# A third buffer for 64-bit weight rows, another place for the second quad, and new numbers for the transfer planner

## The chip, the cores and the metric

One core of a Trainium2 chip runs the whole program in one launch. The metric is device time in microseconds (us); shorter is better. Engines are named as in the profile: PE is TensorE, DVE VectorE, ACT ScalarE, POOL GpSimd, SP SyncE. SP issues all the transfers of this kernel.

## The reference

Attention with a sigmoid in place of the softmax, then two feed-forward layers, over 4 × 448 = 1792 tokens:

```python
scores = scale * np.matmul(q, k.transpose(0, 1, 3, 2)) - np.log(S)   # 4 x 12 heads, S = 448, dim 64
attn = 1.0 / (1.0 + np.exp(-scores))
x = (attn @ v) with the heads side by side                            # 1792 x 768
h = x @ w_in;  x = (s * np.maximum(h, 0.0) ** 2 + b) @ w_out          # layer 1, d_ff 2048
h = x @ w_in2
out = (np.maximum(h, 0.0) + alpha * np.minimum(h, 0.0)) @ w_out2      # layer 2
```

The tokens are float32. The four weight matrices come as float64; they are turned into float32 on the chip, and this conversion is a good part of what the other engines and the transfers do.

## The kernel before, in words

**Phases.** Attention runs until about 136 us, on tiles of 64 × 64, with TensorE multiplying (L857, L895) and ScalarE computing a sigmoid (L873) for each. Then come layer 1 and layer 2, each for two groups of tokens: in, out, in, out, about 103 us each. The first of these, in of layer 1 for the first group, is `first_phase` (about 136 to 245 us): eight blocks `mp` of 7 × 9 = 63 matmuls. The later ones are `in_phase` and `out_phase`.

**Strassen.** Each layer multiplies by Strassen and Winograd's scheme of seven products (M1 to M7) on 2 × 2 blocks. The left operand of a product is one of seven combinations of weight blocks, A11, A12, A22 and S1 to S4. Each float32 operand is split into a high part (ACT, L450, a CAST) and a low part (DVE, L453, a difference), and three matmuls (L547 to L549) stand for one.

**From float64 to a quad.** `quad()` makes the seven combinations for one block. Two loads (L328) bring two rows of 64-bit weights, 768 KB each (512 KB for some), into the two buffers of R64, `r640` and `r641`. For each row ACT runs a Prelu on the high words (L362), DVE joins high and low words into float32 (L365 TENSOR_SCALAR, L370 SCALAR_TENSOR_TENSOR), and DVE forms four sums (L383). The seven results lie side by side in a quad buffer, `quada`, `quadb` or `quadc`, and are stored to DRAM (L402 for in-blocks, L411 for out-blocks: `w0out<-quada`). Later phases load them back as raw units of 512 KB (`raw0`, `raw1`, L328) and split them into `ring`. The first phase doesn't wait for that way round: `direct()` splits straight out of a quad into four buffers `rinq`. Its even blocks stand in quadb, its odd ones in quada. Out-quads of layer 1 that are made early (seven in attention, two inside the first phase) all go through quada.

**Memory.** `quadb` lies over raw0, raw1 and the first part of `neg` (a scratch tensor of layer 2); `quadc` lies at the start of neg.

**The order of the work.** The program first records all operations in `Plan.add`, each with its engine, an estimated duration, a latency, and what it reads and writes. `Plan.order` computes for each the latest start that lets TensorE keep its own order without waiting (`late`), and `Plan.place` then lays the operations down one by one: of what is ready, on the engine that is free first, the one that can start first, and among equals the one due first. It repeats this three times (`ROUNDS`), with TensorE's starts of one pass as the goals of the next. A transfer is reckoned at 345 GB/s (`dma_t`, L314) and a latency of 2.2 us. Loads and stores share one pipe and SP's order. TensorE's own order is fixed as the program records it.

Two kinds of dependence count. Cells of 64 floats give the true ones. Beside them, buffers whose memory overlaps are treated as one by the framework that emits the waits: who comes later in the laid order waits for the last one before it that wrote an overlapping buffer, also where the cells differ. `behind()` (L118) lets the planner reckon with that for an operation which it is about to place, not for those that come after it.

**Buffers of the trace.** `g` holds a layer's result between products, with `L558` (ACT copies out of PSUM), `L568` and `L576` (DVE adds PSUM to g), `L594` (relu), `L629` and `L632` (square, then scale and bias) working on it. `sg` is a sigmoid's result, `x` and `xo` the tokens, `gb` the split g.

Of the kernel before, what the change touches and what calls it, by code (L numbers as in the profile page):

```python
# [16 lines left out]
P = 128  # L17
NWARM = 6
CELL = 64
QUEUES = {"SP": 0.07, "POOL": 1.0}  # L20
AHEAD = 1.0
ROUNDS = 3
SAFE = 0.0
PIPE = {"DVE": 0.08, "ACT": 0.09}
EARLY = 7
# [29 lines left out]
class Plan:  # L55
# [57 lines left out]
    def place(self, succ, late, pe):  # L113
        n = len(self.ops)
        share = self.shared()
        wrote, used = ([{} for _ in share] for _ in range(2))

        def behind(i, eng):  # L118

            x = 0.0  # L120
            for mine, of in zip(self.uses[i], (wrote, used)):
                for t in mine:
                    for o in share[t]:
                        for e, at in of[o].items():
                            if at > x and e != eng:
                                x = at
            return x
        left = [len(op[3]) for op in self.ops]
        est = [0.0] * n
        pe_at = 0  # L130
        open_ = {}
        for i in range(n):
            if left[i] == 0:
                open_.setdefault(self.ops[i][0], set()).add(i)
        free, done, at = {}, [], {}
        pipe = 0.0
        while len(done) < n:
            best = None
            for eng, cand in open_.items():
                if not cand:  # L140
                    continue
                f = free.get(eng, 0.0)
                if eng in QUEUES:
                    f = max(f, pipe - AHEAD)
                if eng == "PE":
                    i = pe[pe_at]
                    if i not in cand:
                        continue
                    est[i] = max(est[i], behind(i, eng))
                    pick = (max(f, est[i]), late[i], i)  # L150
                else:
                    while True:
                        pick = min((max(f, est[i]), late[i], i) for i in cand)
                        i = pick[2]
                        x = behind(i, eng)
                        if x <= pick[0]:
                            break
                        est[i] = x
                if best is None or pick < best[0]:
                    best = (pick, eng)  # L160
            (start, _, i), eng = best
            open_[eng].discard(i)
            if eng == "PE":
                pe_at += 1
            dur, lat = self.ops[i][1:3]
            if eng in QUEUES:
                free[eng] = start + QUEUES[eng]
                pipe = max(pipe, start) + dur
                end = pipe
            else:  # L170
                end = free[eng] = start + dur
            at[i] = start
            done.append(i)
            for k, mine in enumerate(self.uses[i]):
                for t in mine:
                    for of in (used, wrote)[: k + 1]:
                        of[t][eng] = max(of[t].get(eng, 0.0), end + lat)
            for s in succ[i]:
                est[s] = max(est[s], end + (lat if self.ops[s][0] != eng else 0.0) + PIPE.get(eng, 0.0))
                left[s] -= 1  # L180
                if left[s] == 0:
                    open_.setdefault(self.ops[s][0], set()).add(s)
        return done, at
# [26 lines left out]
def tile_kernel(  # L210
# [13 lines left out]
    nc = tc.nc  # L224
    B, NPR, _, SKQ = kq.shape
# [15 lines left out]

    NSLOT = 37
    NRING, NRAW, NTMP = 3, 2, 7
    UNIT = 8 * P
    WQ = KH * P
    base0 = -(-nc.sbuf_base // (4 * CELL)) * CELL
# [5 lines left out]
    def take(n):  # L252
        nonlocal at
        a = at
        at += -(-n // CELL) * CELL
        return a

    def tensor(name, base, n, dtype=F32):
        t = nc.alloc_sbuf_tensor_at(name, [P, n], dtype, offset=4 * base)
        plan.tensors.append((base, base + n))  # L260
        return Ref(t.ap(), base, len(plan.tensors) - 1)

    def own(name, n):
# [1 line left out]

    SLOTS = take(NSLOT * SLOT)
    RING0 = take(NRING * 2 * UNIT)
    PROD = take(8 * WQ + 7 * WQ)
    SPARE = take(NRAW * UNIT + 7 * WQ)
    RING = [tensor(f"ring{i}", RING0 + i * 2 * UNIT, 2 * UNIT, F32R) for i in range(NRING)]  # L270
    RING4 = [tensor(f"rinq{i}", RING0 + i * 4 * WQ, 4 * WQ, F32R) for i in range(4)]
# [1 line left out]
    NEG = tensor("neg", SPARE + NRAW * UNIT, 2 * S)  # L273
# [6 lines left out]
        [(tensor("xraw12", MID + 2 * SLOT + XB, XB), 0, XB)],  # L280
        [(tensor("xraw13", MID + XB, S), 0, S), (tensor("xraw14", NEG.base, 2 * S), S, XB)],
    ]
    R64 = [tensor(f"r64{i}", PROD + 4 * WQ * i, 4 * WQ) for i in range(2)]
    QUADS = [
        tensor("quada", PROD + 8 * WQ, 7 * WQ),
        tensor("quadb", SPARE, 7 * WQ),
        tensor("quadc", NEG.base, 7 * WQ),
    ]
    TMP = [own(f"tmp{i}", S) for i in range(NTMP)]
    SMALL = take(CELL)  # L290
# [21 lines left out]
        return 0.08 + 0.53e-3 * n  # L312

    def dma_t(n):  # L314
        return n * 4 * P / 345e3

    DMA_LAT = 2.2
    PE_LAT = 0.25
# [16 lines left out]
    def quad(m, kind, k, c, place=0):  # L335
# [11 lines left out]
        for row in range(2):  # L347
            src = w64[m, kind][2 * k + row]
            if kind == "out":
                src = src[:, 2 * c0 * P : 2 * c1 * P]  # L350
            r64 = R64[row]
            raw = sb(r64, 4 * n).bitcast(U32)
            load(raw, src.bitcast(U32), 4 * n, (), cells(r64, 4 * n), DMA_LAT + SAFE)
            v = raw.rearrange("p (b n t) -> p b n t", b=2, t=2)
# [57 lines left out]
            cells(QUAD, 7 * n), wrote, DMA_LAT,  # L412
        )

    n_unit = [0, 0]
    ring = {}

    def entry(chunks, ring_=RING):
# [535 lines left out]
    def produce(n, both=False):  # L954
        for i in range(min(n, len(quads))):
            m, kind, k, c, *place = quads.pop(0)
            quad(m, kind, k, c, *(place or [2 * (i % 2) if both else 0]))

    for u in range(NU + 2):
        if u < NU:  # L960
# [89 lines left out]
```

## Time and profile before

| what | us |
|---|---|
| runs | 966.35, 966.47, 974.77 |
| median of the runs | 966.47 |
| the profiled execution | 970.06 |
| its span in the trace | 968.3 |

The span goes from the first to the last instruction in the trace; the execution's own time is 1.76 us longer. The profile has one line per instruction or group, with its start, its duration and, in square brackets, how long the engine had been idle before it and what ended that idle time. `x8` means eight alike in one line. Matmuls overlap in the pipe, so the distance of their starts says more than their durations.

### The profile page before, as it was taken

The page shows a single profiled execution, that of the slowest core. Times are in us where ns is not written, and L with a number is a line of the kernel's source. Part 1 is how long each engine was busy: PE and PEld are TensorE (multiplying, and loading weights), DVE is VectorE, ACT ScalarE, POOL GpSimd, SP SyncE. Part 2 cuts the span into 40 slices and gives each one's busy share as a digit, 9 for nine tenths or more (in the row PEclk, how much of TensorE's full clock was granted, in tenths as well). Part 3 has the DMA queues.
Part 4 walks back from the last instruction along what each step waited for, and adds up shares of the span by engine and source line. Part 5 has one row for each costly group of instructions (what it writes and reads, how often), then busy time and mean ns, then how long its engine had stood idle before and what let it go on. Part 6 is the DMA issues. An engine that isn't in the chain of part 4 may idle for free.

```text
span 968.3 us, 13904 instructions
## 1 busy us (share of the span) xinstructions
PE 954.7 (99%) x5424; PEld 810.4 (84%) x5424; DVE 729.6 (75%) x862; ACT 653.1 (67%) x793; POOL 0.2 (0%) x4
## 2 busy tenths in 40 slices
PE   9999999999999999999999999999999999999998
PEld 4343458988899999998999999999999999999997
DVE  2567648997995877788898969789968556699661
ACT  6989967788945546889946547677555466676451
POOL 0000000000000000000000000000000000000000
PEclk9999999999999999999999999999999999999999
DMA  8999978886663479997567787766444443333441
GB/s 277 343 329 330 348 253 283 291 279 251 213 207 109 145 237 333 311 334 264 190 185 225 252 333 274 247 215 217 148 134 150 138 117 107 103 109 119 133 146 66
DMA packets 81106, 211.68 MB, mean 219 GB/s; under 512 B 7184, under 2 KB 45840, under 8 KB 81040
## 3 DMA queue, kind: packets, MB, share of 16 engines
q1 hardware_dynamic: 81040, 210.80, 65.6%
q8 instruction: 42, 0.69, 0.3%
q14 instruction: 24, 0.20, 0.1%
HBM read 152.97 MB, written 57.80 MB: 218 GB/s over the span
## 4 chain that ended last, share of the span: by engine, by line
PE 67%; DVE 11%; DMA 10%; ACT 8%; issue 3%; SPq 0%; DVEq 0%; ACTq 0%
PE ps L547 20%; PE ps L548 20%; PE ps L549 20%; PE ps L857 4%; DMA w0out<-quada 4%; PE ps L895 3%; DMA r<-in_w_in 3%; DMA r<-in_w_out 3%; DVE ring L453 2%; DVE quada L383 1%; ACT g L629 1%; ACT g L632 1%; DVE quada L370 1%; DVE gb L453 1%; ACT ring L450 1%
## 5 line engine op out<-in xcount | busy, mean ns | idle before, releaser
L547 PE MATMUL ps<-gb,ring 128*128 128x448 f32 x672 | 245.8, 366 | 1.3 <-DVE gb L453 1.3
L549 PE MATMUL ps<-gb,ring 128*128 128x448 f32 x672 | 245.5, 365 | 0.6 <-DVE ring L453 0.6
L548 PE MATMUL ps<-gb,ring 128*128 128x448 f32 x672 | 245.4, 365 | 0.0
L453 DVE TENSOR_TENSOR ring<-raw,ring 128x1024 fp32r<-128x1024 f32 x147 | 179.5, 1221 | 76.5 <-ACT ring L450 76.5
L450 ACT CAST ring<-raw 128x1024 fp32r<-128x1024 f32 x147 | 154.1, 1048 | 100.3 <-PE ps L548 77.5
L547 PE MATMUL ps<-xo,ring 128*128 128x448 f32 x504 | 184.5, 366 | 0.4 <-DVE tmp L568 0.3
L549 PE MATMUL ps<-xo,ring 128*128 128x448 f32 x504 | 184.3, 366 | 0.0
L548 PE MATMUL ps<-xo,ring 128*128 128x448 f32 x504 | 184.3, 366 | 0.0
L547 PEld LDWEIGHTS ps<-gb,ring 128*128 128x128 f32 x672 | 126.2, 188 | 12.5 <-DVE gb L453 2.4
L549 PEld LDWEIGHTS ps<-gb,ring 128*128 128x128 f32 x672 | 126.2, 188 | 11.0 <-DVE ring L453 1.0
L548 PEld LDWEIGHTS ps<-gb,ring 128*128 128x128 f32 x672 | 126.2, 188 | 9.9
L453 DVE TENSOR_TENSOR gb<-g,gb 128x1344 fp32r<-128x1344 f32 (+1 forms) x84 | 116.7, 1399 | 15.2 <-ACT gb L450 13.6
L450 ACT CAST gb<-g 128x1344 fp32r<-128x1344 f32 (+1 forms) x84 | 99.5, 1193 | 25.2 <-PE ps L549 14.6
L547 PEld LDWEIGHTS ps<-xo,ring 128*128 128x128 f32 x504 | 94.6, 188 | 9.0 <-DVE tmp L568 0.6
L549 PEld LDWEIGHTS ps<-xo,ring 128*128 128x128 f32 x504 | 94.7, 188 | 7.8
L548 PEld LDWEIGHTS ps<-xo,ring 128*128 128x128 f32 x504 | 94.7, 188 | 7.8
L873 ACT ACTIVATE sg<-ps,bias 128x896 f32<-128x896 f32 x84 | 83.2, 1010 | 14.7 <-PE ps L857 14.1
L362 ACT ACTIVATE r<-r 128x768 f32<-128x768 f32 (+1 forms) x68 | 59.3, 873 | 42.1 <-DMA r<-in_w_out 23.0
L857 PE MATMUL ps<-kq 64*64 64x448 f32 x672 | 79.6, 548 | 2.8 <-ACT sg L873 2.7
L895 PE MATMUL ps<-sg,v 64*64 64x448 f32 x672 | 77.9, 536 | 0.0
L568 DVE TENSOR_TENSOR g<-ps,g 128x448 f32<-128x448 f32 x104 | 63.5, 620 | 17.3 <-ACT g L558 10.5
L547 PE MATMUL ps<-xo,rinq 128*128 128x448 f32 x168 | 62.5, 372 | 3.8 <-DVE g L568 2.2
(51 smaller groups left out, 994.5 us busy)
## 6 DMA issues: line engine op xcount, KB each, us to landing
r<-in_w_in SPq DMA_DIRECT2D x32, 768.0 KB, 5.9
raw<-w0out SPq DMA_DIRECT2D x42, 512.0 KB, 3.7
raw<-w1in SPq DMA_DIRECT2D x42, 512.0 KB, 3.6
raw<-w1out SPq DMA_DIRECT2D x42, 512.0 KB, 3.6
r<-in_w_out SPq DMA_DIRECT2D x24, 768.0 KB, 5.7
raw<-w0in SPq DMA_DIRECT2D x21, 512.0 KB, 5.7
kq<-in_qk SPq DMA_DIRECT2D x23, 448.0 KB, 5.4
w0out<-quada SPq DMA_DIRECT2D x6, 1344.0 KB, 7.9
```

The costliest lines, as they stand in the source:

```text
L362: nc.scalar.activation(hi, hi, AF.Prelu, scale=2.0**-112, alpha=-(2.0**32))
L370: nc.vector.scalar_tensor_tensor(out=u, in0=hi.bitcast(U32), scalar=3, in1=u, op0=ALU.logical_shift_left, op1=ALU.bitwise_or,)
L383: lambda: nc.vector.tensor_tensor(out=o_, in0=x_, in1=y_, op=op),
L450: add("ACT", act_t(n), lambda: nc.scalar.copy(h, x), cells(src, n), cells(hi, n))
L453: lambda: nc.vector.tensor_tensor(out=l, in0=x, in1=h.bitcast(F32), op=ALU.subtract),
L547: nc.tensor.matmul(d, wh_, ml_, start=first and k == 0, stop=False, **opt)
L548: nc.tensor.matmul(d, wh_, mh_, start=False, stop=False, **opt)
L549: nc.tensor.matmul(d, wl_, mh_, start=False, stop=last and k == n, **opt)
L568: lambda: nc.vector.tensor_tensor(out=d, in0=bank(k), in1=o, op=ALU.add),
L857: nc.tensor.matmul(ps[h * D : (h + 1) * D, k + j, :S], a.ap[rows, S + k0 : S + k0 + D], a.ap[rows, :S], start=True, stop=True,)
L873: lambda: nc.scalar.activation(o, i, AF.Sigmoid, bias=sb(BIAS, 1), scale=QKSCALE),
L895: nc.tensor.matmul(ps[j * D : (j + 1) * D, k + h, :S], va[keys, v : v + D], a.ap[keys, j * S : (j + 1) * S], start=first, stop=last,)
```

## The change

1. R64 gets a third buffer (`NR64 = 3`), and rows take the three in turn instead of one buffer for each of the two rows. The 6 KB of each partition come out of the scratch space for dynamic transfers, which is cut to 1024.
2. `quadb` moves to the start of neg, off the raw units' memory, and `quadc` is gone. Where quads alternate, they alternate between quada and quadb.
3. The planner reckons with 319.4 GB/s instead of 345 and makes one pass instead of three.
4. On SP, an operation that would be picked is set aside when another operation, recorded earlier and not yet placed, uses an overlapping buffer and is due before the transfer would have ended and 4 us more have passed (`POLITE`, `SLACK`, `ahead`).

```diff
+POLITE = ("SP",)
+SLACK = 4.0
-ROUNDS = 3
+ROUNDS = 1
+DMA_RATE = 319.4e3
...
+        def ahead(i, end):
+
+            for mine, of in zip(self.uses[i], open_uses[::-1]):
+                for t in mine:
+                    for o in share[t]:
+                        if any(j < i and late[j] < end for j in of[o]):
+                            return True
+            return False
...
-                        if x <= pick[0]:
-                            break
-                        est[i] = x
+                        if x > pick[0]:
+                            est[i] = x
+                            continue
+                        if eng in POLITE:
+                            dur, lat = self.ops[i][1:3]
+                            x = max(pick[0], pipe) if eng in QUEUES else pick[0]
+                            if ahead(i, x + dur + lat + SLACK):
+                                cand = cand - {i}
+                                if not cand:
+                                    pick = None
+                                    break
+                                continue
+                        break
...
+    NR64 = 3
...
-    PROD = take(8 * WQ + 7 * WQ)
+    PROD = take((4 * NR64 + 7) * WQ)
...
-        tensor("quada", PROD + 8 * WQ, 7 * WQ),
-        tensor("quadb", SPARE, 7 * WQ),
-        tensor("quadc", NEG.base, 7 * WQ),
+        tensor("quada", PROD + 4 * NR64 * WQ, 7 * WQ),
+        tensor("quadb", NEG.base, 7 * WQ),
...
-        return n * 4 * P / 345e3
+        return n * 4 * P / DMA_RATE
...
-            r64 = R64[row]
+            r64 = R64[n_unit[2] % NR64]
+            n_unit[2] += 1
...
-            quad(m, kind, k, c, *(place or [2 * (i % 2) if both else 0]))
+            quad(m, kind, k, c, *(place or [i % 2 if both else 0]))
...
-    nc = bacc.Bacc("TRN2", target_bir_lowering=False, num_devices=1)
+    nc = bacc.Bacc("TRN2", target_bir_lowering=False, num_devices=1, dynamic_dma_scratch_size=1024)
```

The lines of the changed file are 34 or 35 higher than those of the file before (L328 becomes L362, L365 L400, L370 L405, L383 L418, L453 L488, L568 L603). The number of instructions and TensorE's order stay as they are. Three places show what moves.

**SP at the start of attention.** Before, rows 14 to 22 of SP. `r640` and `r641` are the row buffers, `in_w_in1` and `in_w_out1` the weights of layer 1; kq and v are attention's inputs, sc, bc and al small constants:

```order
L328 DMA r641_77<-in_w_in1 128x1536
L328 DMA sc_89<-in_s 128x1
L328 DMA v2_142<-in_vt 128x512
L328 DMA bc_90<-in_b 128x1
L328 DMA al_92<-in_alpha 128x16
L328 DMA r640_76<-in_w_out1 128x1536
L328 DMA kq3_134<-in_qk 128x896
L328 DMA r641_77<-in_w_out1 128x1536
L328 DMA v3_143<-in_vt 128x512
```

and now the same rows:

```order
L362 DMA r642_78<-in_w_out1 128x1536
L362 DMA v2_142<-in_vt 128x512
L362 DMA r641_77<-in_w_in1 128x1536
L362 DMA kq3_134<-in_qk 128x896
L362 DMA r640_76<-in_w_out1 128x1536
L362 DMA v3_143<-in_vt 128x512
L362 DMA kq0_131<-in_qk 128x896
L362 DMA v0_140<-in_vt 128x512
L362 DMA r641_77<-in_w_out1 128x1536
```

The first row of out-weights has moved up by five rows, into the third buffer `r642`; the small loads have left this place, and the third row of out-weights is at row 22.

**DVE between the third and the fourth block of the first phase.** Before, the row in which the third block's last split is made (`rinq3`) and those behind it, up to the fourth block's first split (`rinq0<-quada`):

```order
L453 TENSOR_TENSOR rinq3_66<-quadb_79,rinq3_66 128x384
L365 TENSOR_SCALAR quada_78<-r640_76 128x2x384
L365 TENSOR_SCALAR quada_78<-r641_77 128x2x384
L568 TENSOR_TENSOR g0_114<-ps_95,g0_114 128x448
L370 SCALAR_TENSOR_TENSOR quada_78<-r640_76,quada_78 128x2x384
L370 SCALAR_TENSOR_TENSOR quada_78<-r641_77,quada_78 128x2x384
L568 TENSOR_TENSOR g0_114<-ps_95,g0_114 128x448
L383 TENSOR_TENSOR quada_78<-quada_78 128x384 x4
L453 TENSOR_TENSOR rinq0_63<-quada_78,rinq0_63 128x768
```

and now, from behind that last split to two rows ahead of the fourth block's first:

```order
L400 TENSOR_SCALAR quadb_80<-r640_76 128x2x384
L405 SCALAR_TENSOR_TENSOR quadb_80<-r640_76,quadb_80 128x2x384
L400 TENSOR_SCALAR quada_79<-r641_77 128x2x384
L400 TENSOR_SCALAR quada_79<-r642_78 128x2x384
L405 SCALAR_TENSOR_TENSOR quada_79<-r641_77,quada_79 128x2x384
L405 SCALAR_TENSOR_TENSOR quada_79<-r642_78,quada_79 128x2x384
L418 TENSOR_TENSOR quada_79<-quada_79 128x384
L603 TENSOR_TENSOR g0_114<-ps_95,g0_114 128x448
L418 TENSOR_TENSOR quada_79<-quada_79 128x384
L611 TENSOR_TENSOR g0_114<-g0_114,ps_95 128x448
L418 TENSOR_TENSOR quada_79<-quada_79 128x384
L603 TENSOR_TENSOR g0_114<-ps_95,g0_114 128x448
```

Two operations on quadb, for the block after, have moved ahead of all those on quada, and the sums of PSUM stand between the four L418 instead of ahead of them. Before, they stood behind the fourth block's first two splits.

**SP and the raw units.** Before, the eleven rows around the two loads of raw units, which are the first of the out-phase:

```order
L328 DMA r640_76<-in_w_in1 128x1536
L402 DMA w0in_96<-quadb_79 128x384 x2
L328 DMA r641_77<-in_w_in1 128x1536
L402 DMA w0in_96<-quadb_79 128x384 x5
L328 DMA raw0_67<-w0out_97 128x1024
L402 DMA w0in_96<-quada_78 128x384
L328 DMA r640_76<-in_w_in2 128x1536
L402 DMA w0in_96<-quada_78 128x384
L328 DMA r641_77<-in_w_in2 128x1536
L402 DMA w0in_96<-quada_78 128x384
L328 DMA raw1_68<-w0out_97 128x1024
```

and now the rows around the first of them, some 40 rows sooner:

```order
L446 DMA w0out_97<-quada_79 896x1x256
L362 DMA r640_76<-in_w_in1 128x1536
L362 DMA raw0_67<-w0out_97 128x1024
L763 DMA x01_128<-tmp6_87 128x448
L763 DMA x01_128<-tmp0_81 128x448
L362 DMA r641_77<-in_w_in1 128x1536
L362 DMA r642_78<-in_w_out1 128x1024
L437 DMA w0in_96<-quada_79 128x4x384
L362 DMA r640_76<-in_w_out1 128x1024
L437 DMA w0in_96<-quada_79 128x384 x2
L362 DMA r641_77<-in_w_in1 128x1536
```

The load of `raw0` now stands one load behind the store of an out-quad (`w0out<-quada`) that it reads from, ahead of two stores of x and several rows of weights. The load of `raw1` comes behind these rows, at row 102.

## Rows read from the trace of the kernel before

**Rows 1.** The page, first part: busy us, share of the span, instructions.
```profile
PE 954.7 (99%) x5424; PEld 810.4 (84%) x5424; DVE 729.6 (75%) x862; ACT 653.1 (67%) x793; POOL 0.2 (0%) x4
```
**Rows 2.** Table of waits, PE: waiting line, awaited engine and line: us, times, longest.
```profile
PE ps L857 <- ACT sg L873: 2.7, 3, 2.0
...
PE ps L547 <- DVE g L568: 2.2, 1, 2.2
...
PE ps L547 <- ACT g L558: 1.8, 3, 0.9
...
PE ps L547 <- DVE gb L453: 1.3, 3, 0.7
...
PE ps L549 <- DVE ring L453: 0.6, 1, 0.6
```
**Rows 3.** Stretches: us, busy of PE, PEld, DVE, ACT, POOL; granted clock, DMA share, GB/s.
```profile
0.00:132.00 132.00, 128.13 (x1357) 51.67 (x1361) 71.39 (x103) 112.78 (x135) 0.20 (x4) 1.00 0.91 319
132.00:245.00 113.00, 109.06 (x546) 97.20 (x539) 94.53 (x150) 86.32 (x97) 0.00 (x0) 0.98 0.79 269
347.00:450.00 103.00, 102.83 (x504) 94.11 (x503) 78.82 (x107) 77.74 (x95) 0.00 (x0) 1.00 0.92 309
220.00:230.00 10.00, 7.84 (x31) 6.83 (x30) 5.72 (x9) 7.37 (x8) 0.00 (x0) 0.83 0.99 363
```
**Rows 4.** Timeline of attention, SP, ACT and PE: start, us, what, idle before.
```profile
19.01 0.38 SPq L328 DMA_DIRECT2D r<-in_w_out  x1
...
26.68 0.93 ACT L362 ACTIVATE r<-r 128x768 f32<-128x768 f32 x1 [1.58 <-DMA r<-in_w_out]
...
28.55 0.98 PE L857 MATMUL ps<-kq 64*64 64x448 f32 x8 [1.99 <-ACT sg L873]
```
**Rows 5.** Timeline of the first phase, ACT and PE around two waits.
```profile
164.85 0.89 ACT L362 ACTIVATE r<-r 128x768 f32<-128x768 f32 x1 [1.02 <-DMA r<-in_w_in]
165.65 1.68 ACT L594 ACTIVATE g<-g 128x1792 f32<-128x1792 f32 x1
...
167.80 0.47 PE L547 MATMUL ps<-xo,rinq 128*128 128x448 f32 x1 [0.95 <-ACT g L558]
...
194.34 0.47 PE L547 MATMUL ps<-xo,rinq 128*128 128x448 f32 x1 [0.72 <-ACT g L558]
```
**Rows 6.** Timeline of the first phase, SP, DVE and PE around the first raw unit.
```profile
218.93 0.32 SPq L328 DMA_DIRECT2D raw<-w0out  x1
...
222.95 0.96 DVE L453 TENSOR_TENSOR rinq<-quadb,rinq 128x768 fp32r<-128x768 f32 x1 [3.61 <-DMA raw<-w0out]
...
221.96 0.37 PE L549 MATMUL ps<-xo,rinq 128*128 128x448 f32 x1
224.49 0.47 PE L547 MATMUL ps<-xo,rinq 128*128 128x448 f32 x1 [2.16 <-DVE g L568]
...
225.75 0.58 PE L549 MATMUL ps<-xo,rinq 128*128 128x448 f32 x1
226.13 0.58 PE L547 MATMUL ps<-xo,rinq 128*128 128x448 f32 x1
```
**Rows 7.** Chain of waits, 60 to 260 us, its stores of out-quads: start, us, what.
```profile
131.58 7.59 DMA w0out<-quada
...
161.50 5.66 DMA w0out<-quada
...
192.25 4.07 DMA w0out<-quada
```
**Rows 8.** Timeline of ACT and DVE ahead of the fourth block.
```profile
153.76 0.67 ACT L362 ACTIVATE r<-r 128x512 f32<-128x512 f32 x1 [2.75 <-DMA r<-in_w_out]
...
167.25 1.03 DVE L365 TENSOR_SCALAR quada<-r 128x768 uint32<-128x768 uint32 x2 [2.64 <-DMA w0out<-quada]
...
173.25 1.82 DVE L453 TENSOR_TENSOR rinq<-quada,rinq 128x768 fp32r<-128x768 f32 x2
```
**Rows 9.** Table of waits, ACT on raw units of the first layer's in-phase.
```profile
ACT ring L450 <- DMA raw<-w0in: 3.8, 5, 1.5
```

More of the change, by code (lines that the diff above doesn't have):

```diff
@@ L127, in behind @@
             return x
+        open_uses = [[set() for _ in share] for _ in range(2)]
+        for i, mine in enumerate(self.uses):
+            for k in range(2):
+                for t in mine[k]:
+                    for of in open_uses[: k + 1]:
+                        of[t].add(i)
+        def ahead(i, end):
[5 more added lines that the diff above has]
+            return False
         left = [len(op[3]) for op in self.ops]
@@ L155, in place @@
                         x = behind(i, eng)
-                        if x <= pick[0]:
-                            break
-                        est[i] = x
+                        if x > pick[0]:
[11 more added lines that the diff above has]
+                        break
+                    if pick is None:
+                        continue
                 if best is None or pick < best[0]:
@@ L175, in place @@
                 for t in mine:
+                    for of in open_uses[: k + 1]:
+                        of[t].discard(i)
                     for of in (used, wrote)[: k + 1]:
@@ L282, in tile_kernel @@
     ]
-    R64 = [tensor(f"r64{i}", PROD + 4 * WQ * i, 4 * WQ) for i in range(2)]
+    R64 = [tensor(f"r64{i}", PROD + 4 * WQ * i, 4 * WQ) for i in range(NR64)]
     QUADS = [
-        tensor("quada", PROD + 8 * WQ, 7 * WQ),
-        tensor("quadb", SPARE, 7 * WQ),
-        tensor("quadc", NEG.base, 7 * WQ),
+        tensor("quada", PROD + 4 * NR64 * WQ, 7 * WQ),
+        tensor("quadb", NEG.base, 7 * WQ),
     ]
@@ L413, in quad @@
         )
-    n_unit = [0, 0]
+    n_unit = [0, 0, 0]
     ring = {}
```

## The prediction

> **What bounds the kernel now.** I read the page's first part, then the table of waits, then the table by stretches, then the timeline around each wait. The page shows TensorE busy for 954.7 of 968.3 us [rows 1]. So what a change of buffers and order can give is inside the missing 13.6 us and what the idle time does to the clock. The table of waits names TensorE's waits [rows 2]: 2.7 on ScalarE's sigmoid, 2.2 on VectorE's sums of PSUM, 1.8 on ScalarE's COPY out of PSUM, and 1.3 and 0.6 on splits in the later phases; 8.6 in these five. The starts of the matmuls lose a little more, as the pipe refills after a wait (2.53 from start to start where the row says 2.16, below: I use 0.2 for each wait of the others). By stretches [rows 3], attention has TensorE busy 128.1 of its 132 us, the first layer's first phase 109.1 of 113 with a granted clock of 0.98, and an in-phase that works from raw units 102.8 of 103 for 504 matmuls (0.204 us a matmul). The change can therefore gain in the first 245 us; behind them it can mainly lose.
>
> **Attention: ScalarE behind a late load.** The long waits begin with r: a load is issued at 19.01, its Prelu on ScalarE waits 1.58 and runs 26.68 to 27.61, the sigmoid stands behind it, and TensorE idles 1.99 at 28.55 [rows 4]. The lead from issue to Prelu is 7.7 us. With two buffers a load goes out only when the buffer of two rows ago is free; with three it goes out a row earlier. The order of SP shows it: the first row of out-weights moves from row 19 to row 14, and three small loads no longer stand ahead. I take the 2.7 us of such idle [rows 2] as gone, 3.3 from start to start (0.2 us of refill at each of three). If the loads, which already keep the queues at 0.91 of their time and 319 GB/s [rows 3], come no sooner, the gain is nought; I take the whole, as the rate stays and only the lead grows.
>
> **First phase: ScalarE behind a late load.** At 164.85 a Prelu has waited 1.02 for its row. Behind it stands a relu of 1.68 us, and only then the COPY out of PSUM for which TensorE idles 0.95 at 167.80 [rows 5]. A twin at 194.34 idles 0.72. The third buffer lets the row come before it is needed. With the refill the two are 2.0 us, from nought to 2.0; I take 2.0.
>
> **The raw units' memory.** At 218.93 SP issues the first raw unit, whose memory quadb shares. VectorE's split of a piece of quadb that the load doesn't touch waits for it all the same, 3.61 us, until 222.95: a transfer that was put ahead in the order is waited for by all later users of an overlapping buffer. TensorE's last matmul before starts at 221.96, the next at 224.49: 2.53 apart, 2.33 more than the usual 0.20 [rows 6]. With quadb on the memory of neg no raw unit overlaps it, so this can't recur. Then comes the clock: over 220 to 230 it was 0.83 granted [rows 3], so 3.4 of the ten us ran at the lower level, half of full speed; the matmuls of 225.75 and 226.13 start 0.38 apart [rows 6]. Some nine of them at 0.37 against 0.204 fill that time and cost 1.5 us. I take 3.8, of the range from 2.3 (the fall stays for another reason) to 3.8, since the fall comes a microsecond behind this wait and nothing else near it idles TensorE.
>
> What each of these idle times does to the clock differs: after 1.99 us in attention no matmul was slow, and the stretch has 1.00 [rows 3, 4]; after 2.16 the clock fell to the lower of its two levels (1.2 of 2.4 GHz) for nine matmuls. The Trainium skill ("TensorE: Matmul & The Clock Gate", Part 1, on the clock gate) says that a gap in TensorE's work can throttle it again until activity raises the clock. By that rule the 1.5 us belong to the wait and go with it, by the attention row alone the wait would cost 2.3; the forecast below would read 1.5 later.
>
> **What is gone** is 3.3 + 2.0 + 3.8 = 9.1 us.
>
> **What comes: the fourth block of the first phase.** Its weights are assembled in quada, which until then holds the eighth out-quad, whose store must land first. Three stores of that chain took 7.59, 5.66 and 4.07 us [rows 7]; the middle one holds the fourth block: issued at 161.50, and VectorE begins on quada at 167.25 after 2.64 of waiting. From there two TENSOR_SCALAR, two SCALAR_TENSOR_TENSOR and four sums (with two sums of PSUM between them) bring the first split to 173.25, done at half its 1.82, 174.2: 7.0 us [rows 8]. TensorE is there at 167.80 + 36 × 0.204 = 175.1, so today it doesn't wait. Of the 9.1 gained, 3.3 + 1.1 (2.0 less the twin's 0.9) lie ahead: TensorE comes at 170.7. The chain gets quicker by less. The row that feeds the store waited 2.75 at 153.76 [rows 8]; with that row early I let the store go 1.5 sooner, at 160.0, and land at 165.7. In the new order VectorE does two operations on quadb for the next block first, so it starts on quada near 165.8; 7.0 us on, and with one sum of PSUM more (0.6 or less), the split is ready at 172.8 to 173.2. TensorE waits about 2.3 us, and half of a clock fall like that of 224.49 makes 0.75: I take 3.0, between nought (the store lands 2.3 sooner) and 3.8 (with the whole fall).
>
> The Trainium skill ("DMA: Bandwidth & Descriptors", Anatomy of one DMA) gives a transfer some 2.0 us fixed and its bytes at 436 GB/s, fitted on another path than this queue. By that, an estimate: 1344 KB take 5.2 us and 896 KB 4.1. The trace agrees for the last store (4.07) and not for 7.59, which shared the queues. By the rule's time alone the fourth block's wait would shrink to under one; that is the first rival.
>
> **What costs nothing.** SP now has the first raw unit one load behind an out-quad's store and waits there until that lands (before, it stood behind the last blocks' loads). Behind it on SP are stores of x and the next rows of weights, which the third buffer keeps a row ahead; if that cover is gone, a row is late by up to the 4 to 5.7 us of such a store [rows 7], under the rivals. Smaller scratch costs nothing, as GpSimd, which would use it, is busy for 0.2 us [rows 1]. From about 250 on the orders agree almost wholly; the small waits there, 1.3 and 0.6 us on splits with 0.7 the longest [rows 2], I leave standing. ScalarE waits for raw units of the first layer's in-phase five times, 3.8 us in all, 1.5 the longest [rows 9], and TensorE doesn't feel it.
>
> **Sum.** 970.06 − 9.1 + 3.0 = 963.96 for the profiled execution (span 968.3 and 1.76 around it). That execution was 3.6 above the median of the runs, 966.47; the same difference of 6.1 from the median gives 960.4.
>
> **The rivals.**
> A, the fourth block's wait doesn't come, because stores land sooner with less traffic beside them: 966.47 − 9.1 = 957.4. For it speaks that the last store took 4.07 and that the block before leaves VectorE idle 2.64 [rows 8]; against it the traffic, 0.79 of the queues' time in that phase [rows 3].
> B, the change of order doesn't do what it says outside the conflict of memory: the loads come no sooner, as the queues are full, and what attention gains the chain of stores through quada takes back. Then 2.3 is left: 964.2. For it speaks 0.91 in attention [rows 3]; against it that the Prelu of attention waits 1.58 for a load issued only 7.7 us ahead [rows 4], and that the order puts that load five rows earlier.
> C, slower: the in-phase of 347 to 450 has 0.92 of the queues' time at 309 GB/s [rows 3], and there the third buffer lets rows of 786 KB (2.5 us each) go ahead of raw units. It decides once ScalarE's wait for a unit exceeds the 1.5 us that TensorE doesn't feel [rows 9]. Eight quads with one such row each are 20 us of delay, of which I let half reach TensorE: 966.47 − 6.1 + 10 = 970.4. Against it: the order of SP there is nearly that of before.
>
> **How the numbers follow.** The forecast has 0.50, A 0.20, B 0.22, C 0.08. A measurement of this kernel can tell about 1% from no change, 9.7 us: faster means under 956.8. A's centre lies 0.6 above that line, so I put 0.09 of its 0.20 beyond; of the forecast's 0.50 another 0.09, where half of the new wait and some of the later ones go as well: 0.18. Slower means over 976.1, a third of C: 0.03. The rest, 0.79, is the same. The range goes from 955.0 (A, with the 1.9 of the later splits and 0.5 of refill) to 967.5 (the conflict alone gained, and 3.3 lost to a longer fourth block).
>
> **What would show it.** Right: no wait of TensorE on the sigmoid above 0.3 us before 132; the first phase starting near 132; no split of quadb waiting for a raw unit; a wait of about 2.3 near 171 on a split of quada, with some matmuls 0.37 apart behind it; the granted clock of 1.00 in the ten us before the out-phase, which starts some 6 us sooner. Wrong: sigmoids that still stand behind Prelus waiting for r, a fourth block without a wait (A), or ScalarE's waits for raw units of the in-phase far above 3.8 us (C).

## The result, and the profile after

| | before | after |
|---|---|---|
| median, us | 967.08 (5 runs, 966.35 to 978.19) | 960.51 (5 runs, 960.03 to 960.67) |
| ratio to before | | 0.9878, 95% interval 0.9835 to 0.9921 |
| profiled execution, us | 970.06 | 960.67 |
| its span, us | 968.3 | 958.8 |

The forecast was 960.4. The page's first part [rows 1] and TensorE's table of waits [rows 2] of the changed kernel:

```profile
PE 951.5 (99%) x5424; PEld 810.2 (85%) x5424; DVE 728.6 (76%) x862; ACT 654.3 (68%) x793; POOL 0.2 (0%) x4
```
```profile
PE ps L582 <- DVE gb L488: 1.1, 2, 0.9
PE ps L960 <- DVE bias L966: 1.0, 1, 1.0
PE ps L584 <- DVE rinq L488: 0.8, 1, 0.8
PE ps L582 <- ACT rinq L485: 0.7, 1, 0.7
```

The sigmoid's waits, the COPY's and the 2.2 us on VectorE's sum are no longer there. What is new are two waits on rinq. The stretches [rows 3], with the ten us in which those two lie:

```profile
0.00:132.00 132.00, 130.94 (x1396) 52.82 (x1397) 71.64 (x105) 115.58 (x138) 0.20 (x4) 1.00 0.92 319
132.00:245.00 113.00, 110.53 (x529) 100.08 (x528) 100.50 (x157) 89.01 (x98) 0.00 (x0) 0.98 0.90 305
166.00:176.00 10.00, 8.44 (x33) 7.02 (x33) 9.67 (x16) 9.06 (x10) 0.00 (x0) 0.84 0.98 324
220.00:230.00 10.00, 10.00 (x50) 9.09 (x49) 8.24 (x13) 8.87 (x11) 0.00 (x0) 1.00 0.73 241
347.00:450.00 103.00, 103.00 (x510) 95.43 (x510) 77.87 (x103) 84.21 (x103) 0.00 (x0) 1.00 0.91 314
```

Attention is now nearly full; the ten us of the old conflict have a clock of 1.00, and the clock has fallen somewhere else, at 166 to 176. The timeline of the fourth block, SP, DVE, ACT and PE, and TensorE's last wait before the later phases:

```profile
131.28 0.47 PE L582 MATMUL ps<-xo,rinq 128*128 128x448 f32 x1
...
158.48 0.52 SPq L446 DMA_DIRECT2D w0out<-quada  x1
...
163.79 0.96 DVE L405 SCALAR_TENSOR_TENSOR quadb<-r,quadb 128x768 uint32<-128x768 uint32 x1
164.67 1.02 DVE L400 TENSOR_SCALAR quada<-r 128x768 uint32<-128x768 uint32 x2
...
166.16 3.66 ACT L667 ACTIVATE g<-g,bc,sc 128x1792 f32<-128x1792 f32 x2
...
169.72 2.70 ACT L485 CAST rinq<-quada 128x768 fp32r<-128x768 f32 x4
...
171.07 3.15 DVE L488 TENSOR_TENSOR rinq<-quada,rinq 128x768 fp32r<-128x768 f32 x4
...
170.59 0.47 PE L582 MATMUL ps<-xo,rinq 128*128 128x448 f32 x1 [0.74 <-ACT rinq L485]
...
172.07 0.47 PE L584 MATMUL ps<-xo,rinq 128*128 128x448 f32 x1 [0.81 <-DVE rinq L488]
...
243.16 0.47 PE L582 MATMUL ps<-gb,ring 128*128 128x448 f32 x1 [0.91 <-DVE gb L488]
```

The first phase starts at 131.28 (135.59 before). The store is issued at 158.48; VectorE begins on quada at 164.67, and TensorE, there at 169.7, waits twice.

A ledger from the starts of TensorE's matmuls in the two traces (a step less its usual 0.2 us):

| where | before | after |
|---|---|---|
| start of the program, where both orders are the same | 1.7 | 0.9 |
| attention, the sigmoid | 3.5 | 0.2 |
| first phase, the two waits on the COPY | 2.0 | 0 |
| first phase, conflict with the raw unit | 2.3 | 0 |
| its nine matmuls at the lower clock | 1.5 | 0 |
| fourth block, two waits | 0 | 1.9 |
| its nine matmuls at the lower clock | 0 | 1.5 |
| from 240 us on | 3.3 | 1.4 |

That is 14.3 against 5.9, 8.4 of the 9.5 us by which the spans differ. Most of the rest lies in small steps. The second matmul behind a late start comes 0.31 us after the first in place of 0.20; from the first phase on there are ten such starts before and four now, 0.6 us. And the first phase had one more wait before, 0.26 us at 202.40.

**A second thing in the trace.** At a granted clock of 1.00 TensorE's matmuls follow each other in one of two steps, 0.2027 or 0.2067 us. The same stretch of the same kernel, changed, in this profile and in a later one (e5):

```profile
500.00:700.00 200.00, 200.00 (x989) 185.33 (x988) 178.61 (x211) 131.05 (x170) 0.00 (x0) 1.00 0.69 230
```
```profile
500.00:700.00 200.00, 200.00 (x969) 181.64 (x968) 174.80 (x208) 128.64 (x168) 0.00 (x0) 1.00 0.70 230
```

989 matmuls in 200 us against 969. Over the 3000 matmuls of 242 to 850 us the long step costs some 12 us, twice what the change was forecast to give. In the thirteen profiles read here the step changes 28 times, not counting changes with matmuls at the lower clock between: 26 times at a matmul that had started late, and twice (near 240 us, in e1 and e2) at nothing that shows. So in what follows I give two numbers: the runs as timed, and the profile's span with its stretches of long steps reckoned as short ones (their time by 1 − 0.2027 / 0.2067 = 0.0194 taken off). Reckoned so, before is 968.3 − 66 × 0.0194 = 967.0 and after 958.8 − 66 × 0.0194 = 957.5.

### The profile page after: what moved, and what is told of

Read it like the earlier page. It is cut to its first block, busy times and chain, and to the rows that moved or that the text cites. A ratio compares the mean times of both kernels' runs of the same rounds, so it can differ in the third digit from the quotient of the medians.

```text
span 958.8 us, 13861 instructions
## 1 busy us (share of the span) xinstructions
PE 951.5 (99%) x5424; PEld 810.2 (85%) x5424; DVE 728.6 (76%) x862; ACT 654.3 (68%) x793; POOL 0.2 (0%) x4
## 4 chain that ended last, share of the span: by engine, by line
PE 96%; DVE 3%; issue 0%; ACT 0%; DVEq 0%
PE ps L582 28%; PE ps L584 28%; PE ps L583 27%; PE ps L892 7%; PE ps L930 7%; DVE gb L488 1%; DVE ring L488 0%; DVE g L603 0%; DVE g L498 0%; PE ps L960 0%; DVE quada L418 0%; ACT neg L647 0%; DVE g L652 0%; DVE g L611 0%; ACT g L649 0%
## 5 line engine op out<-in xcount | busy, mean ns | idle before, releaser
L488 DVE TENSOR_TENSOR ring<-raw,ring 128x1024 fp32r<-128x1024 f32 x147 | 179.2, 1219 | 80.1 <-ACT ring L485 79.7
L582 PEld LDWEIGHTS ps<-gb,ring 128*128 128x128 f32 x672 | 126.2, 188 | 11.8 <-DVE gb L488 1.9
L488 DVE TENSOR_TENSOR gb<-g,gb 128x1344 fp32r<-128x1344 f32 (+1 forms) x84 | 116.5, 1396 | 17.2 <-ACT gb L485 13.0
L603 DVE TENSOR_TENSOR g<-ps,g 128x448 f32<-128x448 f32 x104 | 63.9, 620 | 27.6 <-PE ps L584 18.6
L593 ACT COPY g<-ps 128x448 f32<-128x448 f32 x88 | 46.1, 527 | 45.4 <-PE ps L584 45.1
```

What stands on the lines that cost most here:

```text
L488: lambda: nc.vector.tensor_tensor(out=l, in0=x, in1=h.bitcast(F32), op=ALU.subtract),
L582: nc.tensor.matmul(d, wh_, ml_, start=first and k == 0, stop=False, **opt)
L593: nc.scalar.copy(d, bank(k))
L603: lambda: nc.vector.tensor_tensor(out=d, in0=bank(k), in1=o, op=ALU.add),
```

## The experiments

Three parts of the change were tried alone, and each was taken out alone. The polite rule and the one pass got no run. With the set of polite engines empty the changed kernel's order is the same, row for row on every engine, and so is that of the kernel before with one pass instead of three. But beside the other parts they are not idle. With three passes the changed kernel's order is another one, in which VectorE's last split of quadb stands behind a load of x that shares its memory (the conflict that e1 shows below). And the kernels of e3, e4 and e9 have another order without the polite rule. What the two are worth there is not shown.

**e1, the second quad's place alone.**
```diff
-        tensor("quadb", SPARE, 7 * WQ),
-        tensor("quadc", NEG.base, 7 * WQ),
+        tensor("quadb", NEG.base, 7 * WQ),
...
-            quad(m, kind, k, c, *(place or [2 * (i % 2) if both else 0]))
+            quad(m, kind, k, c, *(place or [i % 2 if both else 0]))
```


> The kernel before with one part of the change: quadb on the memory of neg, quadc gone; two row buffers, 345 GB/s and three passes as before. Theory (the conflict of the raw unit with quadb cost 2.3 us of wait and 1.5 us of lower clock, and both go with the memory): 966.5 - 3.8 = 962.7 us; no split of quadb waits for a raw unit, and the ten us before the out-phase have a granted clock of 1.00. The waits in attention (2.7 us on the sigmoid) stay. Rival 1 (the lower clock has another cause): 964.2, clock 0.83 still. Rival 2 (the wait was hidden by another that stands right behind it): 966.5, with a new wait of TensorE of 2 us at the same place.

Measured: 974.88 (969.88 to 978.93, 12 runs) against 971.71 for the kernel before beside it; ratio 1.0026, 0.9994 to 1.0059. Span 977.1, reckoned 966.8. Timeline of SP, DVE and PE:

```profile
219.63 0.32 SPq L327 DMA_DIRECT2D xraw<-x  x1
...
223.48 0.96 DVE L452 TENSOR_TENSOR rinq<-quadb,rinq 128x768 fp32r<-128x768 f32 x1 [3.56 <-DMA xraw<-x]
...
225.02 0.47 PE L546 MATMUL ps<-xo,rinq 128*128 128x448 f32 x1 [2.13 <-DVE g L567]
```

The same split waits as long as before (3.56 for 3.61), now for a load of x: xraw14 lies over the start of neg as well. The wait of 2.13 stands; only the clock didn't fall behind it. My theory of the memory falls.

**e2, the third buffer alone.**
```diff
-    R64 = [tensor(f"r64{i}", PROD + 4 * WQ * i, 4 * WQ) for i in range(2)]
+    R64 = [tensor(f"r64{i}", PROD + 4 * WQ * i, 4 * WQ) for i in range(3)]
...
-            r64 = R64[row]
+            r64 = R64[n_unit[2] % 3]
+            n_unit[2] += 1
...
```


> The kernel before with one part of the change: a third row buffer in turn, and its room; quadb on the raw units' memory, 345 GB/s and three passes as before. Theory: TensorE's waits on the sigmoid in attention go (3.3 us from start to start) and the two waits on the COPY of the first phase (2.0), the wait at the fourth block comes (3.0 to 3.4), the conflict of the raw unit stays: 966.5 - 5.3 + 3.2 = 964.4 us. Rival (the third buffer brings nothing without the planner's lower rate, since loads come no sooner): 966.5, with sigmoid waits of 2.7 us still there.

Measured: 971.94 (967.62 to 982.53, 12 runs) against 971.71; ratio 0.9986, 0.9949 to 1.0022. Span 967.7, reckoned 965.1. The sigmoid's waits fell to 0.4 us and the first phase began at 132.29, as expected. A split of quadb still waited for the raw unit, 2.0 us, but TensorE didn't feel it. It now had this Prelu on ACT and this wait on PE:

```profile
186.80 0.92 ACT L363 ACTIVATE r<-r 128x768 f32<-128x768 f32 x1 [2.61 <-DMA r<-in_w_in]
...
193.31 0.47 PE L548 MATMUL ps<-xo,rinq 128*128 128x448 f32 x1 [2.21 <-ACT g L559]
```

At 345 GB/s the planner thinks that the row is there earlier than it is, and puts its Prelu ahead of a relu and the COPY. A third buffer doesn't mend that. A second new wait, 2.58 us at 248.12, is on a split of gb.

**e3, the changed kernel with two buffers.**
```diff
-    NR64 = 3
+    NR64 = 2
```


> The changed kernel with two row buffers in place of three, all else as changed. Theory: the waits on the sigmoid come back (+3.3 us), so do those on the COPY (+2.0), and as TensorE then comes later to the fourth block, its wait there (3.4 us measured with its lower clock) goes: 960.5 + 5.3 - 3.4 = 962.4 us. Rival (the lower rate in the planner, not the buffer, took the waits of attention away): no wait on the sigmoid above 0.3 us, and 960.5 or less.

Measured: 973.88 (969.49 to 981.97, 12 runs) against 971.71; ratio 1.0021, 0.9985 to 1.0058. Span 978.5, reckoned 966.5. No wait on the sigmoid at all, and the first phase began at 130.99: for attention the rival was right. The loss is in the first phase, which lasts 115.2 us (107.1 in the changed kernel), in PE's waits on rinq:

```profile
PE ps L582 <- ACT rinq L485: 3.9, 3, 1.4
PE ps L584 <- DVE rinq L488: 3.6, 3, 1.2
```

Three blocks, each with two waits. Ahead of the fourth and the sixth block VectorE stood idle (2.78 and 1.95 us) until an out-quad's store had landed:

```profile
168.66 1.03 DVE L400 TENSOR_SCALAR quada<-r 128x768 uint32<-128x768 uint32 x2 [2.78 <-DMA w0out<-quada]
```

With two buffers the out-quad's rows come later, and so its store: the one ahead of the fourth block is issued at 163.1 (158.5 in the changed kernel).

**e4, the changed kernel with 345 GB/s.**
```diff
-DMA_RATE = 319.4e3
+DMA_RATE = 345e3
```


> The changed kernel with the planner reckoning 345 GB/s as before, all else as changed. Theory (third buffer and memory carry the gain, the rate nothing): 960.5 us within 0.7, no wait on the sigmoid above 0.3 us. Rival (only the lower rate makes the planner issue loads early enough): the waits of attention are back, 2.7 us on the sigmoid, 963.8 us or more.

Measured: 966.01 (964.11 to 970.47, 12 runs) against 971.71; ratio 0.9938, 0.991 to 0.9967. Span 968.7, reckoned 965.8. Waits on the sigmoid are 1.5 us, half-way back, and the pattern of e2 is there (ACT, then PE):

```profile
188.53 0.93 ACT L397 ACTIVATE r<-r 128x768 f32<-128x768 f32 x1 [2.58 <-DMA r<-in_w_in]
189.34 1.70 ACT L629 ACTIVATE g<-g 128x1792 f32<-128x1792 f32 x1
...
195.01 0.47 PE L582 MATMUL ps<-xo,rinq 128*128 128x448 f32 x1 [3.09 <-ACT g L593]
```

So the number in the planner, for which my sum had no term, is worth 8 to 9 us in the presence of the other parts.

**e5, the changed kernel again, on the chip of e6 to e8.**

> The changed kernel as it is, beside the others on one chip. In the profiles so far TensorE's matmuls follow each other at one of two steps, 0.2027 or 0.2067 us, at a granted clock of 1.00 either way, and the step changes only behind a wait of TensorE. Theory (a wait draws the step, and the changed kernel has one wait at 242 us that decides the next 610 us): all runs within 0.7 us of 960.4 if that wait always draws the short step, or a second group near 972 (3000 matmuls by 0.004). Rival (the step is the chip's, not the kernel's): runs spread over 960 to 976 as those of the kernel before spread over 965 to 982.

Measured: five runs of 958.21 to 961.53 and seven of 968.28 to 972.61; median 969.47 against 972.26, ratio 0.9931, 0.9889 to 0.9973. The profiled run, 970.67 with a span of 968.8, has the long step from 241.7 to 864.4 (reckoned 956.8). It begins behind this wait of PE, in a place where the first profile had a wait of 0.91 and the short step behind it:

```profile
241.36 0.47 PE L582 MATMUL ps<-gb,ring 128*128 128x448 f32 x1 [1.16 <-DVE gb L488]
```

The five runs after the change on the first chip all lay in the short group. Here both groups come on one chip, so the step isn't the chip's alone. The expectation's "only behind a wait" goes too far: in e1 and e2 the step changed once each at nothing that shows.

**e6, the last two out-quads later.**
```diff
-                if mp % 2 == 1 and EARLY + mp // 2 < len(outs):
-                    quad(*outs[EARLY + mp // 2])
+                if mp in (3, 5):
+                    quad(*outs[EARLY + mp // 2 - 1])
```


> The changed kernel with the last two out-quads of layer 1 made behind the blocks of mp 3 and 5 in place of 1 and 3, so that no store of an out-quad stands between the second and the fourth block in quada. Theory (the fourth block waits for that store): TensorE's two waits of 0.74 and 0.81 us near 170 and the nine matmuls at half clock behind them are gone (3.4 us), 957.1 us; or, if the sixth block takes the wait over, a wait of the same kind near 195 and 960.5. Rival (the fourth block waits for VectorE's order, the sums of PSUM between the sums of the quad, not for the store): waits near 170 of 0.7 us and more remain.

Measured: 956.81 (955.68 to 958.81, 6 runs) against 972.26; ratio 0.9836, 0.9798 to 0.9875. Span 954.5, no stretch with the long step. PE's waits:

```profile
PE ps L960 <- DVE bias L966: 1.0, 1, 1.0
PE ps L582 <- DVE gb L488: 0.9, 2, 0.7
PE ps L582 <- ACT g L593: 0.5, 1, 0.5
```

No wait on rinq is left, in the fourth block or later. Reckoned against reckoned, 954.5 to 957.5 and 956.8, it gains 2.3 to 3.0 us where 3.4 were expected. The waits go with the out-quad. Whether its store made them or the order that is laid around it, this run doesn't tell, as it changes both.

**e7, one wait of TensorE more.**
```diff
                 bk = {"M2": 6 + k % 2, "M5": 3 + k, "M3": 3 + k}.get(x, k)
+                if (m, g, x) == (1, 0, "M2"):
+                    bk = (6, 6, 7)[k]
```


> The changed kernel with one wait of TensorE added: in the out-phase of layer 2, first group, the second product M2 goes into the PSUM bank of the first, so that it waits for VectorE's sum of that bank, near 667 us; nothing else waits between 242 and 854. Theory (a wait draws the step anew): 0.9 us for the wait itself, and behind it until 854 either the short step, 961.3 us in all, or the long one, 920 matmuls by 0.004 us = 3.7 more, 965.0; two groups of runs, or one at either. The profile then shows a step that is new from 667 on. Rival (the step has nothing to do with waits): 961.3 in all runs, the step unchanged at 667.

Measured: five runs of 959.61 to 962.90, three of 966.09 to 968.13. The profiled run was one of the three (966.09, span 964.3, reckoned 960.3). Its added wait and the stretches ahead of and behind it:

```profile
671.10 0.47 PE L582 MATMUL ps<-gb,ring 128*128 128x448 f32 x1 [1.46 <-DVE tmp L603]
```
```profile
500.00:660.00 160.00, 160.00 (x792) 148.26 (x791) 140.76 (x178) 107.60 (x146) 0.00 (x0) 1.00 0.76 256
672.00:850.00 178.00, 178.00 (x880) 164.97 (x879) 123.19 (x123) 101.63 (x129) 0.00 (x0) 1.00 0.42 123
```

The step is the short one on both sides (160 / 792 and 178 / 880, 0.202 both), and this run's long steps lie elsewhere (132 to 243 and behind 858). So this run doesn't show that an added wait makes the step anew; what the others did behind 671 isn't known. Inconclusive.

**e8, 300 GB/s.**
```diff
-DMA_RATE = 319.4e3
+DMA_RATE = 300e3
```


> The changed kernel with the planner reckoning 300 GB/s in place of 319.4. Theory (a lower rate only makes the planner put Preluds and assembly later, and the rows then stand ready): no wait on the sigmoid and no wait of a Prelu above 1 us in the first phase; 960.5 within 1.5, more where the sums of PSUM ahead of the quad's sums delay a block. Rival (the number has to fit the transfers' true rate): waits of 2 us and more in the first phase, 964 or more.

Measured: 974.88 (967.15 to 978.74, 12 runs) against 972.26; ratio 0.9995, 0.9955 to 1.0035. Span 965.4, reckoned 964.7. It has no wait on the sigmoid but one of 5.23 us at the second block. A lower number is no better than a higher one:

```profile
149.54 0.74 PE L582 MATMUL ps<-xo,rinq 128*128 128x448 f32 x1 [5.23 <-ACT rinq L485]
```

**e9, the changed kernel with quadb back.**
```diff
-        tensor("quadb", NEG.base, 7 * WQ),
+        tensor("quadb", SPARE, 7 * WQ),
+        tensor("quadc", NEG.base, 7 * WQ),
...
-            quad(m, kind, k, c, *(place or [i % 2 if both else 0]))
+            quad(m, kind, k, c, *(place or [2 * (i % 2) if both else 0]))
```


> The changed kernel with quadb back over the raw units and quadc at the start of neg, all else as changed: with the runs with two buffers and with 345 GB/s the third of the parts taken out singly. The load of the first raw unit then stands behind all the blocks' rows on SP (row 133 in place of 86). Theory (each part alone carries nearly nothing, but without the memory the conflict is back): a split of quadb waits 2 us or more for a raw unit, TensorE idles 0.7 to 2.2 us near 215 to 222 and the clock may fall behind it; 960.3 + 2.3 to 3.8 with the short step of 0.2027 behind it, some 10 more with the long one. Rival (the planner's lower rate alone keeps the raw units behind quadb's last use): no such wait; the raw units come late instead, and the wait at the start of the out-phase is above 1.5 us.

Measured: 961.79 (960.60 to 973.85, 12 runs, nine of them up to 962.77) against 970.29; ratio 0.9922, 0.9884 to 0.9961. The profiled run has the long step from 131 to 173 and from 244 to 867: span 971.5, reckoned 958.7. No split of quadb waits for a raw unit; SP issues the first at 217.09, when the last split of quadb (213.70) has begun. PE waits 0.64 at the out-phase's start, not more than in the changed kernel. So the conflict stays away, as the rival has it, but without the price it names. That the lower rate alone does this isn't shown: without the polite rule the order of e9 has VectorE's last split of quadb behind the first raw load, and with the rate alone (e10) a CAST of quadb waits 0.41 for a raw unit. What PE pays here are 1.53 and 0.85 at the fourth block and a wait on a COPY. SP's first raw loads, VectorE's first operation on quada for the fourth block, and that wait:

```profile
217.09 0.80 SPq L363 DMA_DIRECT2D raw<-w0out  x2
...
165.05 1.02 DVE L401 TENSOR_SCALAR quada<-r 128x768 uint32<-128x768 uint32 x2
...
230.55 0.47 PE L583 MATMUL ps<-xo,rinq 128*128 128x448 f32 x1 [1.97 <-ACT g L594]
```

**e10, the planner's rate alone.**
```diff
-        return n * 4 * P / 345e3
+        return n * 4 * P / 319.4e3
```


> The kernel before with one part of the change: the planner reckons 319.4 GB/s; two row buffers, quadb over the raw units, three passes. Theory (the lower rate takes the sigmoid's waits away as the third buffer does, but with two buffers the blocks of the first phase come late, as in the changed kernel with two buffers): the first phase starts at 131 to 132 and lasts 112 to 116 us, waits of TensorE on splits of rinq of 1.2 us and more; the profile's span with its long steps reckoned as short ones within 2 us of the kernel before reckoned so (966.9). Rival (the rate alone carries the change): span reckoned so of 958 to 961.

Measured: 974.32 (972.11 to 982.27, 12 runs) against 970.29; ratio 1.0032, 0.9997 to 1.0066. Span 971.8, reckoned 968.9. First phase from 131.07, 117.2 us long (112 to 116 were expected). PE's waits, as in e3, and ACT's on a raw unit:

```profile
PE ps L549 <- DVE rinq L453: 3.6, 3, 1.2
PE ps L547 <- ACT rinq L450: 3.5, 3, 1.6
...
224.56 1.25 ACT L450 CAST rinq<-quadb 128x768 fp32r<-128x768 f32 x2 [0.41 <-DMA raw<-w0out]
```

**e11, e6 once more.**

> The kernel whose last two out-quads of layer 1 are made behind mp 3 and 5, once more. Theory (fewer waits of TensorE mean fewer draws of the step, and its wait near 238 is as short as it was): runs at 955.7 to 958.8 as before, a second group near 968 in less than half of them. Rival (its six runs were lucky draws): as many at 968 as at 957, like the changed kernel's five of twelve.

Measured: five runs of 956.62 to 957.73 and one of 968.24, median 956.87; ratio 0.9859, 0.9814 to 0.9904. Span 955.2. So the long step comes here too, in one run of the twelve of e6 and e11.

**All together** (span of the profiled run with long steps reckoned as short):

| kernel | us | against before |
|---|---|---|
| before | 967.0 | |
| quadb's place alone (e1) | 966.8 | −0.2 |
| third buffer alone (e2) | 965.1 | −1.9 |
| rate alone (e10) | 968.9 | +1.9 |
| all but the third buffer (e3) | 966.5 | −0.5 |
| all but the rate (e4) | 965.8 | −1.2 |
| all but quadb's place (e9) | 958.7 | −8.3 |
| all, two profiles | 957.5, 956.8 | −9.5, −10.2 |
| all, out-quads later (e6, e11) | 954.5, 955.2 | −12.5, −11.8 |

Each number is from one profile. Two profiles of one kernel differ by 0.7, and falls of the clock, some 1.5 us each, are still in them: two in e2, e3 and e10, one in before, e4 and the first profile of all, none in the others. So differences under 2 us, those of e1, e2 and e10 among them, say little. What stands clear is that the third buffer and the rate need each other: without either of them 8 to 10 us of the gain are gone (e3, e4), and alone neither brings it (e2, e10). That the two are enough is not shown, as e9 has the polite rule and the one pass as well.

## Why the prediction was right, and where its steps were not

**Attention: right in size, half right in cause.** 3.3 us were to go and 3.3 went by the ledger. But e3 and e10 have no wait on the sigmoid with two buffers and the lower rate, e2 has nearly none with three and the old rate. So the lower rate is enough there. The third buffer nearly is by itself (e2), but not beside the other parts (e4, 1.5 us).

**The COPY's waits: right in size, wrong in cause.** "The third buffer lets the row come before it is needed" fails in e2 and e4, where a Prelu waits 2.6 us for its row with three buffers. It takes the planner's lower rate to place the Prelu behind the work that TensorE wants, and even that is not enough in every order: e9 and e10, at the lower rate, wait 1.97 and 1.9 us on a COPY. The sum had no term for the rate; it was the larger omission, and rival B, which allowed that the order brings nothing, had the wrong part under suspicion.

**The raw units' memory: right in size, wrong in cause.** "With quadb on the memory of neg no raw unit overlaps it, so this can't recur" is true of raw units and overlooked xraw14 on the same memory (e1). Nor is the move needed for it where the polite rule holds the raw load back (e9). In the changed kernel the load of x is issued at 213.69, after the last split of quadb has begun (213.12), so no split is left to wait. Taking the move back costs 1.2 to 1.9 us of the whole (e9), within the 2 us that single profiles leave open.

**The clock.** The 1.5 us of lower clock went with the conflict and came back with the new wait. Neither is certain. In e1 the wait of 2.13 had no fall behind it; e5, the changed kernel itself, has 1.00 in the ten us in which the first profile has 0.84, with nearly the same two waits (0.74 and 0.95):

```profile
166.00:176.00 10.00, 8.31 (x40) 7.05 (x39) 9.86 (x16) 9.04 (x11) 0.00 (x0) 1.00 0.95 300
```

The Trainium skill ("TensorE: Matmul & The Clock Gate", Part 1) says that a gap can throttle TensorE. The rows agree with "can": of two nearly equal gaps (2.16 before, 2.13 in e1) one did.

**The fourth block: right in place and nearly in size, its cause open.** TensorE was to come at 170.7 and wait 2.3 with 0.75 for the clock; it came at 169.7, waited 1.9 and paid 1.5, 3.4 for 3.0. (From the prediction's own numbers, 165.8 + 7.0 + 0.6, the split is ready by 173.4 at the latest, not 173.2.) The store was issued 1.5 earlier than I had let it go and took 6.1 us (5.66 before), as the table of transfers of 155 to 170 us has it:

```profile
w0out<-quada SPq DMA_DIRECT2D x1, 896.0 KB, 6.1
```

So it landed at 164.6, and VectorE took 7.4 us from there to the first split's end near 172, as long as was reckoned with its added sum. But a sooner store would have gained nothing in that order. VectorE's operation on quadb (163.79, 0.96 us) runs right up to its first one on quada at 164.67, with no idle time between, where before it had stood idle for 2.64 [rows 8]; the same order in e5 has 0.2 us of idle there. Behind that, three sums of PSUM stand between the quad's four sums, and ScalarE comes to the CAST straight from 3.66 us of scale and bias (L667). In e9 the store lands at 164.0, a microsecond ahead of VectorE's start, and TensorE waits longer. So in these runs it is mainly the order on VectorE and ScalarE that holds the block. Whether the planner laid that order because of the store is not shown, as e6 takes away both.

By the Trainium skill's fit ("DMA: Bandwidth & Descriptors", Anatomy of one DMA), made on another path, an estimate for 896 KB is 4.1 us; the 6.1 here doesn't agree. Rival A, which rested on stores landing sooner, didn't come.

**Left standing, and didn't stand.** "The small waits there ... I leave standing": from 240 us on 3.3 us became 1.4. No part of the sum had this gain of 1.9. Nor did it have the 0.8 at the start, where both orders are the same.

**The total.** By pieces 9.1 − 3.0 = 6.1 was forecast, and the same pieces measure 9.1 − 3.4 = 5.7. The ledger's other 2.7 came on top, and one more in small steps; so the profiled execution fell by 9.4 where 6.1 was forecast for it. Against the median, 6.6 was measured and 6.1 forecast. That this is so close has chance in it: the profiled execution of before was 3.6 above the median that the forecast used, and all five runs of the changed kernel drew the short step. On another chip seven of its twelve runs were at 968 to 973.

**Rival C** didn't come: PE has no wait between 243 and 854 us, it is busy for 103.00 of 103 us in the in-phase, and ScalarE's waits for raw units there fell in sum, from 3.8 to 2.5 [rows 9]. The longest rose from 1.5 to 2.5, past the rival's condition, and TensorE didn't feel that either:

```profile
ACT ring L485 <- DMA raw<-w0in: 2.5, 1, 2.5
```

## What to carry to other kernels

An order that a planner lays down hangs on its rate for transfers: with too high a number, work that waits for a load stood ahead of work that TensorE wants (e4), with a lower one a block came late (e8), and the spare buffer paid only with the number between. That number, 319.4, is the rate that the trace shows in attention [rows 3]. Three numbers were tried, and whether it is the fit or a lucky order that made it the best is not shown. A part that leaves the order as it is beside all the others can still matter once one of them is taken out. A buffer that is moved off one conflict has to be looked up against everything on its new place. And a part's worth found by taking it out is not its worth alone; here the parts taken out singly add up to some 19 us (9.0 to 9.7, 8.3 to 9.0 and 1.2 to 1.9) of a gain of 10.

## What the runs showed of the hardware that I had not expected

With 448 columns and a granted clock of 1.00 TensorE has two steps, 0.2027 and 0.2067 us, 2% apart. The step is kept over thousands of matmuls, at 0.76 of the queues' time as at 0.42 (e7), and it changed nearly always (26 of 28 times) where TensorE had started late. Weight loads last 0.188 us in both. Two profiles of the same kernel with the same order (after and e5) differ by 10.0 us of span, mostly in this way, and the groups of runs of e5, e9 and e11 lie as far apart. It would explain why the runs of before scatter over 965 to 983, but only one of them was profiled. What decides which step follows a wait stays open: of the changed kernel's own waits the one of 0.81 was followed by the long step and the one of 0.91 by the short one, and the one run that was to show a draw (e7) kept its step. Whether a version without the wait near 240 us would end the scatter was not tried.
